# Wider gaps between the background stages of a recurrence kernel: rows stored 4 to 5 tenths of a step ahead of the first pair products, restart slots zeroed behind their last reader

## The chip, the cores and the metric

One core of a Trainium2 chip runs the whole program. The metric is the time of one execution in device microseconds, the median over several runs.

## What is computed

A recurrence over 768 time steps for 32 heads (batch 4 times 8 heads, width 40), then a feed-forward layer:

```python
for t in range(S):
    y[:, :, t] = np.einsum('bhd,bhde->bhe', rt, state)
    Sa = np.einsum('bhde,bhe->bhd', state, at)
    state_decay = state * wt[:, :, None, :] - np.einsum('bhd,bhe->bhde', Sa, bt)
    state = state_decay + np.einsum('bhd,bhe->bhde', vt, kt)
# x: y as (3072 tokens, 320)
h = x @ w_in                                  # 320 -> 2048
g = np.where(h >= 1, h, np.where(h <= -1, 0.0, (h + 1) ** 2 / 4))
return g @ w_out                              # 2048 -> 320
```

All in float32; the layer's matrices are split into a rounded part and a rest, so that its products run on rounded operands.

## The kernel before

The 768 time steps are 24 chunks of 32, and the main loop takes one chunk `c` per step for all heads, in two halves of 16 heads. In a chunk the recurrence is a chain of small products (L488 to L554) with evacuations on VectorE and ScalarE between them. Between the chain's stages the layer for earlier tokens is fed to TensorE: first product (`ph`, L603), gate on ScalarE and VectorE (`gt`, L611 to L613), rounding (`gh`, ScalarE L619) and rest (`gl`, GpSimd L620), second product (`po`, L632), which needs both.

Four chunks make a set `s` (0 to 5). What the chain needs of a set is prepared ahead, in three background stages, for sets 2 to 5 all of them this way:

- **rows** (`prelude`): four parts of 8 time steps. For a part, w is copied into `wz` by ScalarE (L247), whose first and last slot of each row of 10 are zero so that one scan can restart there; GpSimd zeroes them (L246). A forward scan on VectorE (`scan`, L221) gives the running product P, a backward one in `wz` its reciprocal. Into `arena` go P (ScalarE, L257), and by GpSimd a times P (L258), k and b times the reciprocal (L267, L274, called `kt` and `bt`). A DMA from GpSimd's queue stores `arena` in DRAM (`scr`, L275), and the next part writes the same `arena` and the same `wz`. The loads of w, a, k and b (`ld_w` and so on) and the copies of r and v from DRAM to DRAM (`copy_rv`, L129) go through SP's queue.
- **ab** (`ab_set`): for each of the set's chunks the rows of a and b are loaded from `scr` into `tiab` (`load_rows`, L290, four DMAs), transposed by VectorE into `ea` (L304, two calls for each half of the heads), multiplied in pairs on TensorE (L313) and copied to `pairs` by ScalarE (L320). There is one `tiab` and one `ea`: the next chunk's load waits for the last transposes.
- **inv** (`invert`): VectorE transposes `pairs` (L332), GpSimd inverts by 31 pairs of small operations on `lw` (L343, L349), and at a set's start `adopt` transposes the result (`tinv`, L357).

The stages are generators that yield costs. `fill` runs four times per step, each time with six portions of the layer, and behind each portion it calls `background`: 24 slots a step. For each stage and set a table gives a window, in tenths of a step:

```python
rows=[(0, 0), (14, 36), (38, 62), (66, 102), (106, 142)],
ab=[(0, 0), (36, 44), (62, 79), (102, 119), (142, 159)],
```

The first pair is set 1, the last set 5. In a window `background` runs each stage as far as its share of the summed cost is due, the most late first; the first and third `fill` of a step get 1.4 shares, the others 0.6 (`SHARE`). `drain` finishes a stage at once where the next needs it. So `ROWS_W`, `AB_W` and the windows alone set where an instruction stands among the others; every engine and SP's queue then runs its own instructions in that order, each waiting for what it needs. Around the fills SP also gets the main loop's loads (`ti` L290, `cg` L423 and L426) and every second step the relayout of Y into X (L574 to L584).

Of the kernel before, what the change touches and what calls it, by code (L numbers as in the profile page):

```python
# [24 lines left out]


WINDOWS = dict(
    rows=[(0, 0), (14, 36), (38, 62), (66, 102), (106, 142)],
    ab=[(0, 0), (36, 44), (62, 79), (102, 119), (142, 159)],
    inv=[(12, 38), (44, 78), (81, 118), (121, 158), (161, 198)],  # L30
)

SHARE = (1.4, 0.6) * 2
SLOTS = len(SHARE)

ROWS_W = (2, 2, 4, 2, 6, 6, 4)
AB_W = (1, 4, 1, 4, 12, 15)
INV_W = 12

# [11 lines left out]
def rwkv_moe_kernel(ctx: ExitStack, tc: tile.TileContext, r, k, v, w, a, b, w_in, w_out, ident_d, mask_d, out):  # L51
    nc = tc.nc
# [27 lines left out]
    wz = const.tile([128, D, 10], F32, name="wz")  # L80
# [20 lines left out]
    srcs = {n: x.rearrange("b h (c t) e -> (b h) c t e", t=L) for n, x in dict(k=k, w=w, a=a, b=b).items()}  # L101

    nc.gpsimd.memset(dz, 0.0)

    def zero(x, row=0):
        z = zero_c[row : row + x.shape[0]]
        nc.scalar.copy(x, (z if len(x.shape) == 2 else z.unsqueeze(1)).broadcast_to(list(x.shape)))

    def pad_rows(x, n):
        for q in (1, 3):  # L110
            zero(x[32 * q : 32 * q + 32, :, n : n + 32], 32 * q)
# [14 lines left out]
    def copy_rv(s, part, c):  # L126

        x, o = ((r, O_R), (v, O_V))[part]
        nc.sync.dma_start(  # L129
            scr4[s][c, :, :, o : o + D], x.rearrange("b h (n t) e -> (b h) n t e", t=L)[:, 4 * s + c]  # L130
        )

    def pad_scr(s):
        nc.sync.dma_start(scr[s][NH * 128 : NH * 128 + 1, 0:D], r[0, 0, 0:1, :])
# [78 lines left out]
    def scan(out, d0, d1, step=1):  # L213


        def line(x):
            x = x.rearrange("p e t -> p (e t)")
            (pp, pn), (st, n) = x.ap
            return x if step == 1 else bass.AP(x.tensor, x.offset + (n - 1) * st, [[pp, pn], [-st, n]])

        nc.vector.tensor_tensor_scan(  # L221
            out=line(out), data0=line(d0), data1=line(d1), initial=0.0, op0=ALU.mult, op1=ALU.add
        )

    def prelude(s):

        reclaim(8)
        R = arena.rearrange("p (t x) -> p t x", x=160)
        kt, P, at, bt = (R[:, :, 40 * i : 40 * i + 40] for i in range(4))
        rows_ = lambda x: x.rearrange("p e t -> p t e")  # L230

        def load(n, part):
            if n == "w":
                t = work.tile([128, 10 * D], F32, tag="ld_w", name="ld_w")
            else:
                t = work.tile([128, 8 * D], F32, tag="ld_x", name=f"ld_{n}", bufs=2)
            x = t[:, 0 : 8 * D].rearrange("p (t e) -> p t e", e=D)
            nc.sync.dma_start(x, srcs[n][:, 4 * s : 4 * s + 4, 8 * part : 8 * part + 8, :])
            return (t, x) if n == "w" else x

        wl, al, kl = load("w", 0), load("a", 0), load("k", 0)
        pad_scr(s)
        yield 10
        for part in range(4):
            ts_ = slice(8 * part, 8 * part + 8)
            nc.gpsimd.memset(wz[:, :, 0::9], 0.0)  # L246
            nc.scalar.copy(rows_(wz)[:, 1:9], wl[1])  # L247
            yield ROWS_W[0]
            Pc = wl[0].rearrange("p (e t) -> p e t", t=10)
            if part == 0:  # L250
                nc.vector.memset(dz[:, :, 0], -1.0)
            scan(Pc, wz, dz)
            yield ROWS_W[1]
            if part < 3:
                nc.vector.tensor_copy(dz[:, :, 0], Pc[:, :, 8])
            nc.vector.reciprocal(dz[:, :, 9], Pc[:, :, 8])
            nc.scalar.copy(P, rows_(Pc)[:, 1:9])  # L257
            nc.gpsimd.tensor_mul(at, al, rows_(Pc)[:, 0:8])  # L258
            yield 1
            scan(wz, wz, dz, -1)  # L260
            rec = rows_(wz)[:, 2:10]
            for i in range(2):
                copy_rv(s, i, part)
            yield ROWS_W[2]
            bl = load("b", part)
            yield ROWS_W[3]
            nc.gpsimd.tensor_mul(kt, kl, rec)  # L267
            if part < 3:
                wl = load("w", part + 1)
            yield ROWS_W[4]  # L270
            if part < 3:
                al = load("a", part + 1)
            yield ROWS_W[5]
            nc.gpsimd.tensor_mul(bt, bl, rec)  # L274
            nc.gpsimd.dma_start(scr[s][0 : NH * 128, 80:240].rearrange("(p t) x -> p t x", t=L)[:, ts_, :], R)  # L275
            yield ROWS_W[6]
            if part < 3:
                kl = load("k", part + 1)
# [13 lines left out]
    def ab_set(s):  # L292

        if 9 in lending:
            reclaim(9)
            pad_rows(tiab, 48)
        load_rows(tiab, 4 * s, O_A, 80)
        yield AB_W[5]
        for c in range(4 * s, 4 * s + 4):
            tv = tiab.rearrange("p h (j x) -> p h j x", x=40)[:, :, :, 0:32]  # L300
            for half in range(2):
                ea = work.tile([128, 8, 2, 32], F32, tag="ea", name="ea")
                for i in range(2):
                    nc.vector.transpose(ea[:, 4 * i : 4 * i + 4], tv[:, 8 * half + 4 * i : 8 * half + 4 * i + 4])  # L304
                    yield AB_W[0]
                yield AB_W[1]
                ps = psum()[:, 0:128]
                for p in range(8):
                    for f in range(2):
                        rows = slice(64 * f, 64 * f + D)  # L310
                        q = 2 * f + p % 2
                        sl = p // 2
                        nc.tensor.matmul(  # L313
                            ps[32 * q : 32 * q + 32, 32 * sl : 32 * sl + 32],
                            lhsT=ea[rows, p, 0, :], rhs=ea[rows, p, 1, :], start=True, stop=True,
                        )
                assert s - 1 in turned_in
                at = 256 * (c % 4) + 128 * half
                yield AB_W[2]
                nc.scalar.copy(pairs_f[:, at : at + 128], ps)  # L320
                yield AB_W[3]
            if c < 4 * s + 3:
                load_rows(tiab, c + 1, O_A, 80)
                yield AB_W[4]
# [35 lines left out]
    def staged(key, needs, work_of):  # L360
# [13 lines left out]
    done, size, spent = dict(rows=1, ab=1), dict(rows=10 + 4 * (1 + sum(ROWS_W)), ab=AB_W[5] + 3 * AB_W[4] + 8 * (2 * AB_W[0] + sum(AB_W[1:4])), inv=INV_W + 67), {}  # L374
    back = {k: staged(*a) for k, a in dict(
        rows=("rows", None, prelude), ab=("ab", "rows", ab_set), inv=("inv", "ab", invert)).items()}

    def drain(key, s):
# [374 lines left out]
    def reclaim(kind):  # L753

        lending.discard(kind)
        while any(x[0] == kind for x in sts.values()):
            next(wgen)
# [208 lines left out]
```

## Time and profile before

| what | value |
|---|---|
| runs | 988.73 to 993.32 us, median 992.13 |
| the profiled execution: time | 995.83 us |
| its span, first to last instruction | 994.0 us |
| TensorE (PE) busy | 718.4 us, 72% |
| VectorE (DVE) busy | 597.6 us, 60% |
| ScalarE (ACT), GpSimd (POOL) busy | 416.1 us, 435.1 us |
| mean granted clock of TensorE | 0.829 |

Busy shares are means over stages that differ: the start without the layer, the steps with background stages, the last steps with the layer and the chain alone. How long an engine stood before an instruction, and for whom, stands in brackets in the timeline, or summed in the list of waits.

### The profile page before, as it was taken

How to read it: one execution, taken by the hardware profiler on the slowest of the kernel's cores; microseconds unless marked ns; L12 is line 12 of the kernel's file. 1: busy time of each engine (PE TensorE's matmuls, PEld its weight loads, DVE VectorE, ACT ScalarE, POOL GpSimd, SP SyncE). 2: the span in 40 equal slices, each digit the busy share in tenths (PEclk: the TensorE clock that was granted, in tenths of full speed). 3: DMA queues.
4: the chain of work that ended last, by engine and by line, in shares of the span. 5: the costliest groups of instructions: out<-in, count | busy, mean ns of one | idle time of the engine just before them, and what ended most of it. 6: DMA issues, size and time to landing. Idle time of an engine off the chain costs nothing.

```text
span 994.0 us, 34830 instructions
## 1 busy us (share of the span) xinstructions
PE 718.4 (72%) x14976; PEld 647.8 (65%) x14976; DVE 597.6 (60%) x1362; ACT 416.1 (42%) x896; POOL 435.1 (44%) x594
## 2 busy tenths in 40 slices
PE   4442413565776687688786588787799999999995
PEld 3231312454676576577676578676789888899894
DVE  5787777562646555477754486754477767677310
ACT  5543343231323433335433345433245555555552
POOL 3301234883224765435853345855225763222332
PEclk9565555576768788779988799988789999999998
DMA  9399966675557756657646666646535453543000
GB/s 295 68 188 267 228 132 136 165 154 106 90 107 168 142 103 125 115 129 165 143 97 121 116 142 154 141 92 125 104 67 104 85 120 69 127 84 72 17 32 14
DMA packets 223161, 121.97 MB, mean 123 GB/s; under 512 B 142824, under 2 KB 214696, under 8 KB 223008
## 3 DMA queue, kind: packets, MB, share of 16 engines
q1 hardware_dynamic: 219808, 108.61, 52.5%
q0 software_dynamic: 3200, 11.14, 3.6%
q8 instruction: 118, 1.93, 0.9%
q14 instruction: 35, 0.29, 0.1%
HBM read 90.54 MB, written 27.53 MB: 119 GB/s over the span
## 4 chain that ended last, share of the span: by engine, by line
PE 35%; DMA 17%; POOL 14%; DVE 11%; SPq 8%; ACT 7%; issue 7%; POOLq 0%; DVEq 0%; ACTq 0%
PE po L632 12%; PE ph L603 9%; POOL gl L620 5%; DMA scr<-arena 5%; PE p L525 4%; DMA tiab<-scr 4%; SPq L290 3%; PE p L514 3%; DMA ti<-scr 3%; POOL lw L343 3%; POOL lw L349 3%; ACT gh L619 2%; PE p L488 2%; PE p L554 2%; ACT cg L509 1%
## 5 line engine op out<-in xcount | busy, mean ns | idle before, releaser
L620 POOL TENSOR_TENSOR gl<-gt,gh 128x512 fp32r<-128x512 f32 x96 | 123.5, 1286 | 333.3 <-ACT gh L619 333.3
L603 PE MATMUL ph<-X,w 120*128 120x256 f32 x1536 | 223.9, 299 | 9.6 <-DMA X<-Y 4.9
L603 PEld LDWEIGHTS ph<-X,w 120*128 120x128 f32 x1536 | 201.6, 200 | 18.9 <-issue 11.3
L632 PE MATMUL po<-wide,gh 128*128 128x320 f32 x768 | 158.9, 330 | 30.8 <-ACT gh L619 30.8
L632 PEld LDWEIGHTS po<-wide,gh 128*128 128x128 f32 x768 | 127.9, 204 | 33.8 <-ACT gh L619 33.1
L613 DVE SCALAR_TENSOR_TENSOR gt<-gt,ph 128x512 f32<-128x512 f32 x96 | 65.8, 685 | 115.4 <-ACT gt L612 91.2
L632 PE MATMUL po<-wide,gl 128*128 128x320 f32 x384 | 100.1, 345 | 31.8 <-POOL gl L620 31.5
L532 DVE SCALAR_TENSOR_TENSOR cg<-p,pr 40x160 f32<-40x160 f32 x184 | 59.2, 322 | 82.7 <-PE p L525 80.7
L509 ACT ACTIVATE cg<-p 32x160 f32<-32x160 f32 x192 | 56.6, 295 | 106.0 <-PE p L498 78.7
L611 ACT ACTIVATE gt<-ph,half_c 128x512 f32<-128x512 f32 x96 | 66.0, 688 | 80.9 <-PE ph L603 80.8
L632 PEld LDWEIGHTS po<-wide,gl 128*128 128x128 f32 x384 | 68.3, 207 | 42.1 <-POOL gl L620 41.8
L349 POOL TENSOR_TENSOR lw<-lw 128x31 f32<-128x31 f32 (+15 forms) x155 | 90.2, 582 | 8.0
L466 DVE TENSOR_TENSOR cg<-p,mask 32x256 f32<-32x256 f32 x192 | 80.6, 420 | 14.5 <-PE p L457 11.2
L343 POOL TENSOR_TENSOR lw<-lw 128x31 f32<-128x31 f32 (+15 forms) x155 | 82.2, 531 | 8.5
L514 PE MATMUL p<-cg 128*40 128x40 f32 x1472 | 47.0, 231 | 43.4 <-ACT cg L509 43.4
L514 PEld LDWEIGHTS p<-cg 128*40 128x40 f32 x1472 | 40.6, 143 | 54.5 <-ACT cg L509 44.4
L519 ACT COPY ss<-p 40x320 f32<-40x320 f32 x92 | 38.6, 419 | 87.9 <-PE p L514 86.6
L525 PE MATMUL p<-cg 128*64 128x72 f32 (+1 forms) x1536 | 69.7, 253 | 0.2 <-issue 0.2
L505 DVE SCALAR_TENSOR_TENSOR cg<-p,mask 32x128 f32<-32x128 f32 x192 | 55.3, 288 | 16.0 <-ACT cg L509 9.1
L525 PEld LDWEIGHTS p<-cg 128*64 128x64 f32 x1536 | 64.1, 161 | 0.7 <-issue 0.5
L619 ACT CAST gh<-gt 128x512 fp32r<-128x512 f32 x96 | 59.7, 622 | 10.6 <-DVE gt L613 8.6
L313 PE MATMUL p<-ea 40*32 40x32 f32 x1024 | 19.3, 215 | 61.9 <-DVE ea L304 61.5
(108 smaller groups left out, 1083.8 us busy)
## 6 DMA issues: line engine op xcount, KB each, us to landing
ti<-scr SPq DMA_DIRECT2D x96, 200.0 KB
ti<-scr SPq DMA_DIRECT2D x96, 168.0 KB
scr<-arena POOLq DMA_DIRECT2D x16, 640.0 KB, 5.8
cg<-scr SPq DMA_DIRECT2D x96, 80.0 KB
X<-Y SPq DMA_DIRECT2D x36, 160.0 KB
scr<-wide SPq DMA_DIRECT2D x8, 640.0 KB
tiab<-scr SPq DMA_DIRECT2D x32, 160.0 KB
scr<-in_r_dram SPq DMA_DIRECT2D x24, 160.0 KB
```

What stands on the lines that cost most here:

```text
L343: eng.tensor_mul(t3, W3[:, 0:n, j : j + 1].broadcast_to([128, n, m]), L3[:, j + 1 :, j].unsqueeze(1).broadcast_to([128, n, m]),)
L349: eng.tensor_sub(W3[:, 0:n, j + 1 :], W3[:, 0:n, j + 1 :], t3)
L466: nc.vector.tensor_tensor(out=cg[q, f::2, C_X : C_X + 64][:, 4 * i : 4 * i + 4].rearrange("p h (j x) -> p h j x", x=32), in0=ps[quarter(f, ...
L509: nc.scalar.mul(cg[q, f + 2 * j :: 4, C_S : C_S + D], psv[j][quarter(f, j), :, 32:72], -1.0)
L514: nc.tensor.matmul(pst[er[h % 2], h // 2, :], lhsT=cg[:, h, C_S : C_S + D], rhs=cg[:, h, C_G : C_G + D], start=True, stop=True)
L525: nc.tensor.matmul(psv[h // 8][64 * f : 64 * f + 64, h // 2 % 4, 0:n3], lhsT=cgw[:, h * CW + C_G : h * CW + C_G + 64], rhs=cg[:, h, C_R : ...
L603: nc.tensor.matmul(phs[k % 2][:, n * j : n * j + n], lhsT=w1[:, wi, fs], rhs=Xs[g][:, xi, :], start=i == 0, stop=i == 7)
L611: nc.scalar.activation(gt, ph, AF.Relu, bias=half_c, scale=0.5)
L613: nc.vector.scalar_tensor_tensor(out=gt, in0=gt, scalar=1.0, in1=ph, op0=ALU.min, op1=ALU.max)
L619: nc.scalar.copy(gh, gt)
L620: nc.gpsimd.tensor_sub(gl, gt, gh.bitcast(F32))
L632: nc.tensor.matmul(pos[i], lhsT=x[:, ts_], rhs=w, start=at, stop=end)
```

## The change

Four edits. The windows of rows end 3 to 4 tenths of a step earlier, and set 2's also begins 2 earlier; those of ab begin 1 later. The last cost in `ROWS_W`, behind the store, is 8 instead of 4, which makes a set's rows cost 134 instead of 118. The zeroing of `wz` stands behind bt and the store, where `wz` was read last, with one more at the program's start. And the copy to `pairs` follows its products without a yield between.

```diff
--- before.py
+++ after.py
@@ -25,15 +25,15 @@
 
 
 WINDOWS = dict(
-    rows=[(0, 0), (14, 36), (38, 62), (66, 102), (106, 142)],
-    ab=[(0, 0), (36, 44), (62, 79), (102, 119), (142, 159)],
-    inv=[(12, 38), (44, 78), (81, 118), (121, 158), (161, 198)],
+    rows=[(0, 0), (12, 33), (38, 58), (66, 98), (106, 138)],
+    ab=[(0, 0), (37, 46), (63, 79), (103, 119), (143, 159)],
+    inv=[(12, 36), (47, 78), (81, 118), (121, 158), (161, 198)],
 )
 
 SHARE = (1.4, 0.6) * 2
 SLOTS = len(SHARE)
 
-ROWS_W = (2, 2, 4, 2, 6, 6, 4)
+ROWS_W = (2, 2, 4, 2, 6, 6, 8)
 AB_W = (1, 4, 1, 4, 12, 15)
 INV_W = 12
 
@@ -101,6 +101,7 @@
     srcs = {n: x.rearrange("b h (c t) e -> (b h) c t e", t=L) for n, x in dict(k=k, w=w, a=a, b=b).items()}
 
     nc.gpsimd.memset(dz, 0.0)
+    nc.gpsimd.memset(wz[:, :, 0::9], 0.0)
 
     def zero(x, row=0):
         z = zero_c[row : row + x.shape[0]]
@@ -243,7 +244,6 @@
         yield 10
         for part in range(4):
             ts_ = slice(8 * part, 8 * part + 8)
-            nc.gpsimd.memset(wz[:, :, 0::9], 0.0)
             nc.scalar.copy(rows_(wz)[:, 1:9], wl[1])
             yield ROWS_W[0]
             Pc = wl[0].rearrange("p (e t) -> p e t", t=10)
@@ -273,6 +273,7 @@
             yield ROWS_W[5]
             nc.gpsimd.tensor_mul(bt, bl, rec)
             nc.gpsimd.dma_start(scr[s][0 : NH * 128, 80:240].rearrange("(p t) x -> p t x", t=L)[:, ts_, :], R)
+            nc.gpsimd.memset(wz[:, :, 0::9], 0.0)
             yield ROWS_W[6]
             if part < 3:
                 kl = load("k", part + 1)
@@ -316,9 +317,8 @@
                         )
                 assert s - 1 in turned_in
                 at = 256 * (c % 4) + 128 * half
-                yield AB_W[2]
                 nc.scalar.copy(pairs_f[:, at : at + 128], ps)
-                yield AB_W[3]
+                yield AB_W[2] + AB_W[3]
             if c < 4 * s + 3:
                 load_rows(tiab, c + 1, O_A, 80)
                 yield AB_W[4]
```

On GpSimd, in set 3 from the third part's bt to the fourth part's a times P (`arena<-ld_a`; the `lw` rows are the inversion), before:

```order
L274 TENSOR_TENSOR arena_78<-ld_b_3528,wz_79 128x8x40
L275 DMA scr3_103<-arena_78 128x8x160
L343 TENSOR_TENSOR lw_84<-lw_84 128x207
L349 TENSOR_TENSOR lw_84<-lw_84 128x9x23
L246 MEMSET wz_79 128x40x2
L343 TENSOR_TENSOR lw_84<-lw_84 128x220
L349 TENSOR_TENSOR lw_84<-lw_84 128x10x22
L258 TENSOR_TENSOR arena_78<-ld_a_3640,ld_w_3543 128x8x40
```

and after:

```order
L274 TENSOR_TENSOR arena_78<-ld_b_3394,wz_79 128x8x40
L275 DMA scr3_103<-arena_78 128x8x160
L276 MEMSET wz_79 128x40x2
L343 TENSOR_TENSOR lw_84<-lw_84 128x60
L545 TENSOR_TENSOR Y_889<-yt_3325,Y_889 128x2x4x32
L620 TENSOR_TENSOR gl_3523<-gt_3404,gh_3522 128x512
L349 TENSOR_TENSOR lw_84<-lw_84 128x2x30
L343 TENSOR_TENSOR lw_84<-lw_84 128x87
L349 TENSOR_TENSOR lw_84<-lw_84 128x3x29
L258 TENSOR_TENSOR arena_78<-ld_a_3412,ld_w_3402 128x8x40
```

The zeroing stands directly behind the store instead of two inversion operations later, and two products' rests and a copy of Y now lie between the store and the next part's product.

On SP's queue at set 3's first load of `tiab` (`ti` and `cg` are the chain's loads for the next chunks, `X0<-Y` the relayout), before:

```order
L238 DMA ld_b_3804<-in_b_dram 128x1x320
L290 DMA tiab_81<-scr3_103 32x16x80
L290 DMA tiab_81<-scr3_103 32x16x48
L290 DMA tiab_81<-scr3_103 32x16x80
L290 DMA tiab_81<-scr3_103 32x16x48
L290 DMA ti1_83<-scr1_101 32x8x200
L290 DMA ti1_83<-scr1_101 32x8x168
L290 DMA ti1_83<-scr1_101 32x8x200
L290 DMA ti1_83<-scr1_101 32x8x168
L423 DMA cg2_87<-scr1_101 32x8x80
L426 DMA cg2_87<-scr1_101 32x8x40
```

and after:

```order
L291 DMA ti1_83<-scr1_101 32x8x200
L291 DMA ti1_83<-scr1_101 32x8x168
L423 DMA cg2_87<-scr1_101 32x8x80
L426 DMA cg2_87<-scr1_101 32x8x40
L423 DMA cg2_87<-scr1_101 32x8x80
L426 DMA cg2_87<-scr1_101 32x8x40
L291 DMA tiab_81<-scr3_103 32x16x80
L291 DMA tiab_81<-scr3_103 32x16x48
L291 DMA tiab_81<-scr3_103 32x16x80
L291 DMA tiab_81<-scr3_103 32x16x48
L574 DMA X0_1865<-Y_889 40x1024 x3
```

The load of b, the last part's, is no longer ahead of the `tiab` load; the loads of `ti` and `cg` now are, and the relayout follows directly.

On VectorE in set 2, from the second chunk's last transposes to the third chunk's first (each half of a chunk is one `ea` row here; `gt` is the layer's gate), before:

```order
L304 STREAM_TRANSPOSE ea_2660<-tiab_81 128x256 x2
L532 SCALAR_TENSOR_TENSOR cg0_85<-p2_2683,pr1_89 40x4x40 x2
L532 SCALAR_TENSOR_TENSOR cg0_85<-p2_2684,pr1_89 40x4x40 x2
L537 TENSOR_TENSOR yt_2685<-p2_2683,pr1_89 128x128
L537 TENSOR_TENSOR yt_2685<-p2_2684,pr1_89 128x128
L357 STREAM_TRANSPOSE tinv_107<-lw_84 128x32x32
L445 STREAM_TRANSPOSE ev_2728<-ti1_83 128x512
L447 STREAM_TRANSPOSE pr0_88<-ti1_83 128x16x32
L304 STREAM_TRANSPOSE ea_2775<-tiab_81 128x256 x2
```

and after:

```order
L305 STREAM_TRANSPOSE ea_2724<-tiab_81 128x256 x2
L251 MEMSET dz_80 128x40
L222 SCALAR_TENSOR_TENSOR ld_w_2569<-wz_79,dz_80 128x400
L255 COPY dz_80<-ld_w_2569 128x40
L256 RECIPROCAL dz_80<-ld_w_2569 128x40
L222 SCALAR_TENSOR_TENSOR wz_79<-wz_79,dz_80 128x400
L305 STREAM_TRANSPOSE ea_2759<-tiab_81 128x256 x2
L613 SCALAR_TENSOR_TENSOR gt_2764<-gt_2764,ph1_64 128x512
L305 STREAM_TRANSPOSE ea_2807<-tiab_81 128x256 x2
```

Between the last `ea` of the second chunk and the first of the third stood a stage of the chain, the `tinv` transpose and two transposes of the next chunk; now one gate stands there, and scans stand ahead of it.

## Rows read from the trace of the kernel before

**Rows 1.** The page's second part: TensorE's granted clock in 40 slices of 24.85 us, in tenths of full speed (5 is the lower level, 1.2 GHz).

```profile
PEclk9565555576768788779988799988789999999998
```

**Rows 2.** Timeline of VectorE: the `tinv` transposes at the starts of sets 1, 2 and 3 (start us, duration us, engine, line).

```profile
262.02 2.09 DVE L357 STREAM_TRANSPOSE tinv<-lw 128x1024 f32<-128x1024 f32 x1
...
440.50 2.14 DVE L357 STREAM_TRANSPOSE tinv<-lw 128x1024 f32<-128x1024 f32 x1
...
587.80 2.13 DVE L357 STREAM_TRANSPOSE tinv<-lw 128x1024 f32<-128x1024 f32 x1
```

**Rows 3.** The list of waits over the span: who waited for whom, us in total, times, longest us (SPq is SP's DMA queue).

```profile
PE p L313 <- DVE ea L304: 61.5, 17, 11.2
...
DVE ea L304 <- DMA tiab<-scr: 57.9, 12, 9.5
...
ACT arena L257 <- DMA scr<-arena: 29.6, 6, 5.6
...
DVE ld_w L221 <- POOL wz L246: 24.7, 7, 5.9
...
SPq L290 <- DMA scr<-arena: 69.7, 4, 19.1
```

**Rows 4.** Timeline of TensorE in the rows of sets 2 and 3: start us, duration us, and in brackets the time it stood before and for whom. The last row is four products with no gap ahead, for the clock.

```profile
183.36 1.54 PE L514 MATMUL p<-cg 128*40 128x40 f32 x31 [5.76 <-ACT cg L509]
...
221.38 1.43 PE L632 MATMUL po<-wide,gh 128*128 128x320 f32 x4 [6.67 <-ACT gh L619]
224.76 0.90 PE L632 MATMUL po<-wide,gl 128*128 128x320 f32 x2 [1.94 <-POOL gl L620]
...
305.67 1.44 PE L632 MATMUL po<-wide,gh 128*128 128x320 f32 x4 [4.84 <-ACT gh L619]
...
325.32 1.43 PE L632 MATMUL po<-wide,gh 128*128 128x320 f32 x4 [5.37 <-ACT gh L619]
...
346.47 1.44 PE L632 MATMUL po<-wide,gh 128*128 128x320 f32 x4 [6.52 <-ACT gh L619]
...
355.61 0.75 PE L632 MATMUL po<-wide,gh 128*128 128x320 f32 x4
```

**Rows 5.** Timeline of GpSimd, VectorE and ScalarE from the third part's bt of set 3 to the fourth part's copy of P.

```profile
336.00 1.04 POOL L274 TENSOR_TENSOR arena<-ld_b,wz 128x320 f32<-128x320 f32 x1
...
337.33 0.93 POOL L275 DMA_DIRECT2D scr<-arena  x1 [0.30 <-POOL arena L274]
...
339.46 0.21 POOL L246 MEMSET wz<- 128x80 f32 x1
...
339.71 1.31 DVE L221 TENSOR_TENSOR_SCAN ld_w<-wz,dz 128x400 f32<-128x400 f32 x1 [3.50 <-POOL wz L246]
...
343.46 0.77 ACT L257 COPY arena<-ld_w 128x320 f32<-128x320 f32 x1 [5.62 <-DMA scr<-arena]
```

**Rows 6.** The chain of work that ended last: start and length of two stores, from GpSimd's issue to the landing; the first with other transfers beside it, the second nearly alone.

```profile
211.63 6.68 DMA scr<-arena
...
359.25 4.20 DMA scr<-arena
```

**Rows 7.** Timeline around the first loads of `tiab`: set 2's last store, first transposes and first pair products; set 3's load on SP and first transposes; and TensorE's gaps there in sets 3, 4 and 5.

```profile
235.73 0.93 POOL L275 DMA_DIRECT2D scr<-arena  x1 [0.30 <-POOL arena L274]
...
245.25 0.77 DVE L304 STREAM_TRANSPOSE ea<-tiab 128x256 f32<-128x256 f32 x2 [9.50 <-DMA tiab<-scr]
...
245.84 0.68 PE L313 MATMUL p<-ea 40*32 40x32 f32 x32 [11.23 <-DVE ea L304]
...
363.60 1.90 SPq L290 DMA_DIRECT2D tiab<-scr  x4
...
365.10 0.90 PE L632 MATMUL po<-wide,gl 128*128 128x320 f32 x2 [3.71 <-POOL gl L620]
...
368.68 0.77 DVE L304 STREAM_TRANSPOSE ea<-tiab 128x256 f32<-128x256 f32 x2 [5.71 <-DMA tiab<-scr]
...
513.53 0.57 PE L632 MATMUL po<-wide,gl 128*128 128x320 f32 x2 [3.01 <-POOL gl L620]
...
663.46 0.56 PE L632 MATMUL po<-wide,gl 128*128 128x320 f32 x2 [3.48 <-POOL gl L620]
```

**Rows 8.** Timeline at later loads: set 2's third chunk on VectorE; in set 3 SP's relayout and load of the second chunk; TensorE's gaps before the second chunk (sets 3, 4, 5) and the third (set 3, at 406.40).

```profile
265.68 0.77 DVE L304 STREAM_TRANSPOSE ea<-tiab 128x256 f32<-128x256 f32 x2 [0.43 <-DMA tiab<-scr]
...
369.61 2.46 SPq L574 DMA_DIRECT2D X<-Y  x3
...
380.49 2.00 SPq L290 DMA_DIRECT2D tiab<-scr  x4
...
387.01 0.96 PE L313 MATMUL p<-ea 40*32 40x32 f32 x32 [5.68 <-DVE ea L304]
...
406.40 0.68 PE L313 MATMUL p<-ea 40*32 40x32 f32 x32 [7.95 <-DVE ea L304]
...
536.55 0.67 PE L313 MATMUL p<-ea 40*32 40x32 f32 x32 [5.36 <-DVE ea L304]
...
682.74 0.67 PE L313 MATMUL p<-ea 40*32 40x32 f32 x32 [3.33 <-DVE ea L304]
```

**Rows 9.** Timeline: the load of b for set 3's last part on SP, and the bt that uses it on GpSimd.

```profile
346.58 0.58 SPq L238 DMA_DIRECT2D ld_b<-in_b_dram  x1
...
357.91 1.04 POOL L274 TENSOR_TENSOR arena<-ld_b,wz 128x320 f32<-128x320 f32 x1
```

## The prediction

> **What bounds the kernel now.** No engine is full, so I read where each waits. First the granted clock by slices: up to slice 9 (224 us) TensorE is mostly at or near its lower level, then between the two, and from slice 32 on near full [rows 1]. Then the step times: the four chunk steps between the tinv transposes of sets 1 and 2 took 178.5 us, 44.6 each, the next four 147.3, or 36.8 each [rows 2]. A tenth of a step, the unit of WINDOWS, is therefore about 3.7 to 4.5 us, and one of the 24 background slots of a step 1.5 to 1.9 us. Then the list of waits [rows 3]: TensorE stood 61.5 us before the pair products for VectorE's ea, VectorE 57.9 us before the same ea for the tiab load, the SP queue 69.7 us for four stores of rows, ScalarE 29.6 us for six stores to let go of the arena, VectorE 24.7 us for the zeroing of wz on GpSimd. Every queue is in order, so these count only where TensorE stands too, and the timeline of TensorE says where. I look for its gaps there, and sum those that the edits touch.
>
> **Gaps behind the rows of sets 2 and 3.** Six gaps before the second product, 5.76, 6.67, 1.94, 4.84, 5.37 and 6.52 us, are 31.1 us [rows 4]. One of them in full: bt starts on GpSimd at 336.00, the store at 337.33, the zeroing only at 339.46, behind a pair of inversion operations; the forward scan of the next part stood 3.50 us for it; then ScalarE's copy of P stood 5.62 us until 343.46, because P goes into the arena that the store still reads [rows 5]. Everything behind on ScalarE waits too: the rounding gh, and with it TensorE.
>
> After the change the zeroing follows the store directly, so the scan needs no more from GpSimd. And 8 cost units instead of 4 stand behind the store. By the planner's table worked through, in sets 2 and 3 the copy of P stood 2 to 3 slots behind the store of the part before; it will stand 6 to 7. Six slots at 1.5 us are 9 us, or 6.8 at 27 us a step if most stalls vanish; needed are bt's 1.04, 0.3 to the store, and its landing. The landings on the chain were 4.20 us where the store ran alone and 6.68 in traffic [rows 6], so 5.5 to 8.0 us are needed. At the worst 1.2 us per part stay, some 6 us in all: **-25** (bounds 0 and -31). The Trainium skill, page "DMA: Bandwidth & Descriptors", section on the anatomy of one GpSimd DMA, fits 2.0 us plus bytes over 436 GB/s, an estimate of 3.5 us for the 640 KB. No store here was that quick (4.2 us at best), so the trace decides; by the page nothing would stay and the sum would be 6 us better.
>
> **First load of each set.** In set 2 the last store goes at 235.73, ea waits until 245.25, and TensorE stands 11.23 us [rows 7]. The store and the load of tiab are in neighbouring slots, so the load's wait for the landing holds SP, and VectorE behind it. After, set 2's store goes at about 31.7 tenths and the load at 36.7, five tenths or 18 us apart; sets 3 to 5 six to seven apart (56.7 and 62.9 in set 3). The store has long landed. What the load still needs is its own way: 363.60 to 368.68, 5.1 us [rows 7]. SP may send it before its slot is reached, since it then waits for nothing but the DMAs ahead of it: **-10** of the 11.23 (bounds 0 and -11).
>
> In sets 3 to 5 VectorE's first wait lies beside TensorE's work: there TensorE stood 3.71, 3.01 and 3.48 us, for gl on a GpSimd that had just done bt and the store [rows 7]. Those two move away; the lag of the inversion stays, and the same pair now lags elsewhere. I take a bit over half of the 10.2 us: **-6** (bounds 0 and -10).
>
> **Second load of sets 3 to 5.** TensorE stood 5.68, 5.36 and 3.33 us, 14.4 in all, for the second chunk's ea [rows 8]. In set 3 SP sent the relayout of Y only at 369.61, behind the late tiab, ti and cg, then the loads of the next set's rows, and tiab only at 380.49 [rows 8]. Without the stall at the first load SP is some 5 us earlier there, and the second chunk's ea moves three slots back (from 67.5 to 68.75 tenths), about 5 us more. Ten us against the 4 to 6 that lacked: **-12**, 2.4 left (bounds 0 and -14.4).
>
> **Third load.** Here I see no gain. In set 3 TensorE stood 7.95 us [rows 8]; load and ea stay two slots apart. The new order takes scans out from between the two transposes, so that only one gate is cover, but their time falls ahead of the load instead. I take **+3** for sets 3 to 5 (bounds 0 and +12, 4 us of lost cover each). In set 2 that wait was 0.43 us [rows 8] because a whole chain stage and the tinv transpose lay between. Now one gate does, while the fourth chunk, whose wait was a like one, gets the chain stage: about 5 lost, 4 won, **+1**.
>
> **Denser rows.** The windows of rows shrink from 22, 24, 36 and 36 tenths to 21, 20, 32 and 32, and the cost goes from 118 to 134, so between the load of b and its use in bt there are 3 to 4 slots instead of 7 to 8 in sets 2 and 3. The trace shows no wait at bt: the load went at 346.58 and bt ran at 357.91, 11.3 us later [rows 9]. Half of that, 5.6, meets a landing of about 5.1 if I take the tiab load's for it; a wait of 0 to 2 us in eight parts is 0 to 16 us of GpSimd, and I take **+4** on TensorE. The 17 zeroings instead of 16, and the pair copy that loses its one unit of delay, I cost at nothing: ScalarE stands behind the same products either way.
>
> **Clock.** Behind a gap four products took 1.44 us, without one 0.75 [rows 4]. About ten gaps fewer at 0.5 us each: **-5** (bounds 0 and -10).
>
> Sum: -25 -10 -6 -12 +3 +1 +4 -5 = -50. The profiled execution had a span of 994.0 and a time of 995.83; the median of the runs is 992.13, 0.4% less. I subtract from the median: **942**. With every bound at its best -76, or 916; with half the gaps coming back as other waits, -25, or 967.
>
> **The rivals.**
> The stall moves on (0.14): the third load loses its cover fully, 4 us more in each of four sets, and SP, now with the loads of b and w ahead of that tiab load, cures the second load only by half, 6 us less: 942 + 13 + 6 is about 961. For it speaks that VectorE has one gate between the two transposes; against, that the scans only changed sides.
>
> The first load comes late anyway (0.08): in sets 3 to 5 it now stands behind eight ti and cg DMAs, and if SP is held there for the turn that frees ti, the load is issued where it was. Then -10 and -6 fall to a quarter, and -12 to a half: 942 + 12 + 6 = 960.
>
> The store lands sooner once its neighbours are spread (0.08): 4.2 us for all of them [rows 6], nothing left of the 31.1: 936. The page named above points this way.
>
> No change (0.07): TensorE stands at other waits for the same time, since ScalarE's and GpSimd's chain from gate to gl was only hidden behind the stalls: within 5 us of 992. Against it: the four steps with rows but hardly a gap of this kind took 147.3 us where those with them took 178.5 [rows 2].
>
> **Slower** (0.07): bt waits for its load. SP sends b behind the copies of r and v, and where ti and cg loads or the relayout are ahead by 4 us more; landing 5.1 + 4 against 5.6 leaves 3.5 us on GpSimd in each of 16 parts, and gl behind it holds TensorE: 942 + 56 = 998. It decides from about 3.1 us per part on. Against it stands that b is held only by GpSimd's product at, three slots earlier, and that no bt waited before.
>
> **How the numbers follow.** My forecast has 0.56, with a range of its own from 925 to 958. Faster by over 0.5% (5 us, about what a measurement of this kernel can tell from no change): 0.56 + 0.14 + 0.08 + 0.08 = 0.86. Same 0.07, slower 0.07. The range of 918 to 972 takes in the gaining rivals and nearly all bounds of the terms; it leaves out the last two cases and a little of the forecast's tails.
>
> **What would show it.** Right: no wait of ea for the first tiab load in set 2; SP's 69.7 us for stores gone; ScalarE's 29.6 for the arena under 8; VectorE's 24.7 for wz near 0; no gap of over 2 us at the second chunk; steps of sets 1 to 2 near 38 us. A gap of 5 to 8 us at the third chunk of every set stays. Wrong: bt waiting for ld_b on GpSimd, gaps of po for gl where there were none, or the first ea still waiting because SP stood at the ti loads.

## The result, and the profile after

| | before | after |
|---|---|---|
| runs, median | 991.46 us (988.73 to 993.32) | 930.36 us (926.37 to 932.97) |
| ratio, 95% interval | | 0.938 (0.934 to 0.943) |
| span of the profiled execution | 994.0 us | 930.4 us |
| TensorE busy, mean granted clock | 718.4 us, 0.829 | 700.9 us, 0.863 |

The median before is that of four runs; the prediction's 992.13 was the median of three of them. A run of 2069.08 us, one of twelve of the kernel with the zeroing alone moved, is left out of every median and ratio below.

The forecast was 942, its own range 925 to 958. First the granted clock by slices (of 23.3 us) of the page after, against [rows 1]: 24 of the 40 slices stand at 0.9 or more, where 15 did before.

```profile
PEclk9565655666969897899999799899999999999998
```

The list of waits after, against [rows 3]: VectorE's wait for the zeroing and SP's for the store are nearly gone, ScalarE's for the arena is only halved, and bt has a wait that was not there.

```profile
PE p L314 <- DVE ea L305: 30.6, 22, 3.5
...
DVE ea L305 <- DMA tiab<-scr: 19.4, 4, 6.0
...
ACT arena L257 <- DMA scr<-arena: 15.4, 3, 5.9
...
DVE ld_w L222 <- POOL wz L276: 3.0, 1, 3.0
...
SPq L291 <- DMA scr<-arena: 8.8, 1, 8.8
...
POOL arena L274 <- DMA ld_b<-in_b_dram: 5.2, 2, 3.8
```

Where the time went, by stretches from one tinv transpose to the next, first before, then after. A row: stretch, its length, then busy us and instructions of PE, PEld, DVE, ACT and POOL, the granted clock, the DMA share and GB/s. The first row of each runs from a product of the chain that both kernels start at the same time, 227.2 us, to the end of step 3; the others are steps 4 to 7, 8 to 11 and 12 to 15.

```profile
227.20:262.02 34.82, 22.44 (x479) 20.45 (x478) 13.72 (x36) 9.96 (x23) 7.01 (x12) 0.70 0.55 102
262.02:440.50 178.48, 127.92 (x2659) 115.30 (x2658) 99.39 (x228) 64.75 (x142) 83.47 (x115) 0.79 0.61 125
440.50:587.80 147.30, 114.13 (x2497) 103.30 (x2496) 92.26 (x211) 60.55 (x133) 78.33 (x108) 0.90 0.63 130
587.80:732.90 145.10, 121.72 (x2500) 110.56 (x2499) 86.67 (x202) 58.26 (x129) 71.88 (x101) 0.86 0.55 113
```

```profile
227.20:248.58 21.38, 19.37 (x447) 18.05 (x447) 12.06 (x32) 9.69 (x22) 3.29 (x3) 0.83 0.52 103
248.58:410.11 161.53, 127.43 (x2691) 114.55 (x2690) 102.31 (x232) 64.94 (x143) 84.26 (x115) 0.85 0.68 141
410.11:543.13 133.02, 113.07 (x2499) 102.27 (x2498) 91.99 (x211) 60.90 (x133) 77.24 (x108) 0.92 0.67 144
543.13:669.80 126.67, 109.80 (x2499) 99.06 (x2498) 85.86 (x202) 57.94 (x129) 70.06 (x101) 0.96 0.62 128
```

The first four steps gave 13.4 us (262.02 to 248.58), all of it behind 227.2 us; the next three stretches gave 17.0, 14.3 and 18.4. Steps 16 to 19 gave nothing (105.46 and 105.51 us): of the background stages only the last set's inversion runs there, in a window that the change leaves as it was. In steps 12 to 15 two thirds of the gain are not gaps: TensorE was busy 121.7 us before and 109.8 after with the same instructions, at a clock of 0.86 and 0.96.

The gaps of TensorE after that answer to [rows 4], [rows 7] and [rows 8]:

```profile
210.47 1.43 PE L632 MATMUL po<-wide,gh 128*128 128x320 f32 x4 [5.94 <-ACT gh L619]
...
224.80 0.90 PE L632 MATMUL po<-wide,gl 128*128 128x320 f32 x2 [3.67 <-POOL gl L620]
...
241.34 0.68 PE L314 MATMUL p<-ea 40*32 40x32 f32 x32 [2.01 <-DVE ea L305]
...
310.13 0.90 PE L632 MATMUL po<-wide,gl 128*128 128x320 f32 x2 [5.72 <-POOL gl L620]
...
329.11 0.56 PE L632 MATMUL po<-wide,gl 128*128 128x320 f32 x2 [3.85 <-POOL gl L620]
...
351.44 0.56 PE L314 MATMUL p<-ea 40*32 40x32 f32 x32 [0.93 <-DVE ea L305]
...
367.06 0.33 PE L314 MATMUL p<-ea 40*32 40x32 f32 x16 [1.02 <-DVE ea L305]
...
383.47 0.46 PE L314 MATMUL p<-ea 40*32 40x32 f32 x32 [2.40 <-DVE cg L556]
...
463.44 0.90 PE L632 MATMUL po<-wide,gl 128*128 128x320 f32 x2 [3.44 <-POOL gl L620]
...
515.90 0.66 PE L314 MATMUL p<-ea 40*32 40x32 f32 x32 [4.57 <-DVE cg L556]
...
596.97 0.90 PE L632 MATMUL po<-wide,gl 128*128 128x320 f32 x2 [3.92 <-POOL gl L620]
...
645.11 0.54 PE L314 MATMUL p<-ea 40*32 40x32 f32 x32 [2.61 <-DVE cg L556]
```

The first load of set 2 (241.34) and the second chunk of set 3 (367.06) went as forecast, and the third chunk (383.47), from which I expected nothing, fell from 7.95 to 2.40; in sets 4 and 5 (515.90, 645.11) it fell too, from these gaps before:

```profile
555.80 0.67 PE L313 MATMUL p<-ea 40*32 40x32 f32 x32 [7.65 <-DVE ea L304]
...
699.13 0.68 PE L313 MATMUL p<-ea 40*32 40x32 f32 x32 [4.66 <-DVE ea L304]
```

Behind the rows of set 2 (up to 224.80) nothing is won.

### The profile page after: what moved, and what is told of

The parts are those of the page before. It is cut to its first block, busy times and chain, and to the rows that moved or that the text cites. A ratio compares the mean times of both kernels' runs of the same rounds, so it can differ in the third digit from the quotient of the medians.

```text
span 930.4 us, 34829 instructions
## 1 busy us (share of the span) xinstructions
PE 700.9 (75%) x14976; PEld 631.4 (68%) x14976; DVE 597.2 (64%) x1362; ACT 416.0 (45%) x896; POOL 432.9 (47%) x595
## 4 chain that ended last, share of the span: by engine, by line
PE 31%; POOL 10%; DVE 7%; ACT 5%; issue 4%; DMA 2%; SPq 1%; POOLq 0%; DVEq 0%; ACTq 0%
PE po L632 11%; PE ph L603 8%; POOL gl L620 5%; PE p L525 4%; PE p L514 3%; PE p L488 2%; ACT gh L619 2%; PE p L554 2%; DMA tiab<-scr 2%; DVE cg L556 2%; DVE cg L505 1%; POOL lw L343 1%; POOL lw L349 1%; ACT cg L509 1%; ACT gt L611 1%
## 5 line engine op out<-in xcount | busy, mean ns | idle before, releaser
L603 PE MATMUL ph<-X,w 120*128 120x256 f32 x1536 | 220.0, 295 | 1.3 <-issue 0.8
L603 PEld LDWEIGHTS ph<-X,w 120*128 120x128 f32 x1536 | 197.4, 196 | 9.0 <-issue 1.2
L509 ACT ACTIVATE cg<-p 32x160 f32<-32x160 f32 x192 | 56.6, 295 | 112.9 <-PE p L498 69.7
L349 POOL TENSOR_TENSOR lw<-lw 128x31 f32<-128x31 f32 (+15 forms) x155 | 89.8, 579 | 9.1
L343 POOL TENSOR_TENSOR lw<-lw 128x31 f32<-128x31 f32 (+15 forms) x155 | 79.7, 514 | 8.6
L514 PE MATMUL p<-cg 128*40 128x40 f32 x1472 | 44.7, 224 | 43.2 <-ACT cg L509 43.0
L514 PEld LDWEIGHTS p<-cg 128*40 128x40 f32 x1472 | 38.4, 137 | 53.0 <-ACT cg L509 44.0
L525 PE MATMUL p<-cg 128*64 128x72 f32 (+1 forms) x1536 | 66.6, 247 | 0.0
L554 PE MATMUL p<-pr,ss 40*40 40x32 f32 x1472 | 40.6, 208 | 34.5 <-DVE pr L447 28.7
L554 PEld LDWEIGHTS p<-pr,ss 40*40 40x40 f32 x1472 | 35.5, 128 | 43.4 <-issue 19.8
L619 ACT CAST gh<-gt 128x512 fp32r<-128x512 f32 x96 | 59.7, 622 | 10.7 <-DVE gt L613 8.6
L612 ACT ACTIVATE gt<-gt 128x512 f32<-128x512 f32 x96 | 60.6, 632 | 3.0
```

What stands on the lines that cost most here:

```text
L343: eng.tensor_mul(t3, W3[:, 0:n, j : j + 1].broadcast_to([128, n, m]), L3[:, j + 1 :, j].unsqueeze(1).broadcast_to([128, n, m]),)
L349: eng.tensor_sub(W3[:, 0:n, j + 1 :], W3[:, 0:n, j + 1 :], t3)
L509: nc.scalar.mul(cg[q, f + 2 * j :: 4, C_S : C_S + D], psv[j][quarter(f, j), :, 32:72], -1.0)
L514: nc.tensor.matmul(pst[er[h % 2], h // 2, :], lhsT=cg[:, h, C_S : C_S + D], rhs=cg[:, h, C_G : C_G + D], start=True, stop=True)
L525: nc.tensor.matmul(psv[h // 8][64 * f : 64 * f + 64, h // 2 % 4, 0:n3], lhsT=cgw[:, h * CW + C_G : h * CW + C_G + 64], rhs=cg[:, h, C_R : ...
L554: nc.tensor.matmul(psv[er[f], p, :], lhsT=ss[er[f], p, :], rhs=pn[er[f], p, 0, 8:40], start=True, stop=True)
```

## The experiments

Theory A is that of the prediction with its terms re-sized by the trace after; the rivals stand in the expectations. Each ratio is against the kernel before on the same chip.

**The windows alone.** Only the three tables, as in the diff of the change.

> The kernel before with the three changed tables of windows alone; costs, zeroing and the copy to pairs stay as they were. By the table worked through, the copy of P then stands 5 to 6 slots behind the store of the part before in set 2 and 4 to 5 in set 3 (2 to 3 before, 6 to 7 with the whole change), and all of ab stands as in the whole change. Theory A, that the windows bring most: the first load of set 2 (9 us), the second and third loads of sets 3 to 5 (12 and 11 us) and half of what the rows' gaps gave (5 us) go, with some 6 us of clock: about 948, between 938 and 954; VectorE still waits for the zeroing, and ScalarE still for the store in some parts of set 3. Theory B, that zeroing and cost carry the gain, since every engine ran behind the scan that waited: 975 or more.

Measured: 944.66 us, ratio 0.956 (0.951 to 0.960): 4.4% of the 6.2. Theory A holds, B falls. The first load of set 2 has a gap of 1.99 us. What lacks to the whole change is mostly in steps 8 to 11 (143.1 us against 133.0): in set 4 the old cost leaves the copy of P only 4 slots behind the first store, and the rounding gh is late there. Timeline of TensorE:

```profile
448.23 1.44 PE L632 MATMUL po<-wide,gh 128*128 128x320 f32 x4 [7.42 <-ACT gh L619]
```

The three tables changed together, and two windows of the inversion are among them (set 1's ends 2 tenths earlier, set 2's begins 3 later). No run moves these alone, so their part in the 4.4% is not shown.

**Cost and zeroing alone.**

```diff
-ROWS_W = (2, 2, 4, 2, 6, 6, 4)
+ROWS_W = (2, 2, 4, 2, 6, 6, 8)
```

with the zeroing moved as in the change, the windows as before.

> The kernel before with the last cost of rows 8 instead of 4 and the zeroing moved behind the store, windows and copy to pairs as before. The copy of P stands 4 to 5 slots behind the store in sets 2 and 3; the first load of tiab stays 2 slots behind the last store. Theory A: only part of the rows' gaps go (31 us before; the whole change left about 20), so 8 to 15 us, with clock: about 978, between 970 and 986; the 11 us at the first load of set 2 and the 8 us at the third load of set 3 stay in the trace. Theory B (zeroing and cost carry the gain): 950 or less.

Measured: 974.65 us, ratio 0.985 (0.980 to 0.991). As A expected; 4.4% and 1.5% nearly make up the whole. The first load of set 2 and the third chunk of set 3 stall as before (lines are one further down here):

```profile
240.62 0.68 PE L314 MATMUL p<-ea 40*32 40x32 f32 x32 [10.37 <-DVE ea L305]
...
396.46 0.67 PE L314 MATMUL p<-ea 40*32 40x32 f32 x32 [7.67 <-DVE ea L305]
```

**The zeroing alone.** The memset moved behind the store, nothing else.

> The kernel before with the zeroing of wz alone moved. VectorE's 24.7 us of waiting for it should go to near nothing. Theory A: the scan then runs earlier, but the copy of P still waits for the store that reads the arena, in the same place on ScalarE: the same waits with another name, within 4 us of before (987 to 993). Theory B: the scan's lateness was what made the copy late: 10 us or more gained (982 or less).

Measured: 989.60 us, ratio 1.001 (0.998 to 1.005). A holds. The scan still waits for the zeroing, 20.1 us in all, since bt ahead of it is as late as it was; where it comes earlier, ScalarE stands longer for the store. Set 3, third and fourth part, VectorE and ScalarE:

```profile
312.30 1.04 DVE L222 TENSOR_TENSOR_SCAN ld_w<-wz,dz 128x400 f32<-128x400 f32 x1 [1.15 <-POOL wz L276]
...
317.38 0.76 ACT L257 COPY arena<-ld_w 128x320 f32<-128x320 f32 x1 [5.77 <-DMA scr<-arena]
```

**The pair products early again.** The whole change, with ab's windows of before.

```diff
-    ab=[(0, 0), (37, 46), (63, 79), (103, 119), (143, 159)],
+    ab=[(0, 0), (36, 44), (62, 79), (102, 119), (142, 159)],
```

> The whole change, but with the windows of ab as before (they begin and end up to 2 tenths of a step earlier). The last store still stands 10 to 13 slots ahead of the first load of tiab, but the first pair products of the third chunk stand ahead of the chain's stage at 2.5 tenths of the step again, and those of the second chunk about three slots earlier. Theory A, that the third load's gap shrank since the chain's products of that stage now stand on TensorE between load and pair products: gaps of 6 to 8 us at the third chunk of sets 3 to 5 come back, and half of those at the second: 15 us more than the whole change, 940 to 950. Theory C, that SP being early after an unhindered first load made both gaps small: within 4 us of the whole change, 927 to 934.

Measured: 947.09 us, ratio 0.958 (0.953 to 0.963), 2.0 points of the gain lost. A holds, C falls. The third chunks of sets 3 to 5 have 9.19, 8.15 and 5.94 us again (20.3 before, 9.6 with the whole change), the second chunks 1.41, 3.38 and 1.41. TensorE at the third chunk of set 3, here and then in the whole change:

```profile
382.64 0.67 PE L314 MATMUL p<-ea 40*32 40x32 f32 x32 [9.19 <-DVE ea L305]
383.24 1.28 PE L554 MATMUL p<-pr,ss 40*40 40x32 f32 x32
384.45 1.18 PE L498 MATMUL p<-x,tinv 32*32 32x72 f32 x32
```

```profile
377.45 0.80 PE L554 MATMUL p<-pr,ss 40*40 40x32 f32 x32
378.18 0.70 PE L498 MATMUL p<-x,tinv 32*32 32x72 f32 x32
```

In set 2 the gap at the first load stays small here (1.62 us), although its pair products stand where they stood before. So it was not moving them that removed it, nor cost and zeroing, which left 10.37: that leaves the other windows, those of rows first of all. In both kernels set 3's third load stands two slots ahead of ea. But a window that begins one tenth later puts the pair products behind the chain's stage (L554, L498 and on) instead of ahead of it, so the chain runs while the load is under way. The same instructions take 1.28 and 1.18 us behind the gap, 0.80 and 0.70 without.

**b straight into the arena.** The whole change, with four loads into the arena where there was one into a shared tile.

```diff
-            bl = load("b", part)
+            for i in range(4):
+                nc.sync.dma_start(bt[i::4], srcs["b"][:, 4 * s + i, 8 * part : 8 * part + 8, :])
...
-            nc.gpsimd.tensor_mul(bt, bl, rec)
+            nc.gpsimd.tensor_mul(bt, bt, rec)
```

> The whole change, and b is loaded straight into its quarter of the arena (four DMAs, one for each chunk of the set, where there was one into a tile shared with a and k), so that its load no longer waits for GpSimd's product a times P. Theory A, that the 5.72 us gap of TensorE in set 3 and the 5.2 us that bt stood for its load come from that shared tile: both go, and with them the copy of P that then came 5 us too early for the late store; 5 to 9 us less than the whole change, 921 to 926. Theory D, that what counts is the way of the load itself, which now is four DMAs in rows of 160 bytes: bt waits as long or longer, and the time stays at 930 or goes up to 940.

Measured: 935.12 us, ratio 0.947 (0.942 to 0.951), slower than the whole change (0.938, on another chip). D holds: from SP's issue to bt it was 6.6 us (296.05 to 302.69) against 5.4 with the one load (300.09 to 305.49), bt waited 4.97 us where it had waited 3.81, and TensorE's gap was 6.88 us. GpSimd:

```profile
302.69 1.04 POOL L275 TENSOR_TENSOR arena<-arena,wz 128x320 f32<-128x320 f32 x1 [4.97 <-DMA arena<-in_b_dram]
```

**bt on VectorE.** `nc.gpsimd.tensor_mul(bt, ...)` becomes `nc.vector.tensor_mul`.

> The whole change, with the product bt on VectorE instead of GpSimd; the store stays on GpSimd. Theory A, that the gaps of 3.85, 3.44 and 3.92 us behind the last store of sets 3 to 5 come from the 2.2 us of bt, store and zeroing that stand on GpSimd between the rounding gh and the rest gl: each gap shrinks by 1.0 to 1.3 us, and so do like ones of other parts; 3 to 8 us less than the whole change, 922 to 927. Theory E, that GpSimd is late by the whole inversion and not by the rows' operations: the gaps stay within 0.5 us, and the time within 3 us of 930. If VectorE has to wait for the load of b as GpSimd did (5.2 us in set 3), part of the gain goes, and its other work with it: up to 935.

Measured: 925.30 us, ratio 0.938 (0.934 to 0.942), as the whole change. The gaps at the last stores of sets 3 to 5 fall to 3.08, 2.55 and 2.91 us, so GpSimd's bt is in them, as A has it, but the gain in time that A expected did not come. In set 3 the gap of 5.72 us for gl became one of 5.16 for gh, and VectorE pays the rest back at the load of b, 7.4 us at the longest (list of waits):

```profile
DVE arena L274 <- DMA ld_b<-in_b_dram: 15.5, 3, 7.4
```

**Loads of tiab one slot earlier.** `AB_W = (1, 4, 1, 4, 16, 15)`.

> The whole change, with the cost behind a load of tiab 16 instead of 12. The pair products stand where they stood, but the second, third and fourth load of tiab come one slot earlier, three slots ahead of ea instead of two. Theory A, that at the third chunk of sets 3 to 5 the gaps that are left (2.40, 4.57 and 2.61 us) are the load's own way, of which ea still waits 4 to 6 us: they shrink by about the slot's 1.5 us each, 4 to 6 us less than the whole change, 924 to 927. Theory F, that the SP queue sends the load later anyway, since the loads of rows stand ahead of it: no change within 2 us.

Measured: 929.61 us, ratio 0.943 (0.938 to 0.947). A missed, and the loads go as F has it: SP sent the third loads 6.33, 5.98 and 6.52 us ahead of their transposes, no earlier than in the repeat of the whole change below (6.25, 6.49, 6.81). In set 3 the load of b stood on SP just ahead, 2.71 us long. The third chunks' gaps are 1.79, 3.01 and 1.72 us, but those of the second and fourth of sets 3 and 4 rose from 0.9 to 1.8 us to 2.1 to 2.9: the wait moved to its neighbours.

**Set 3's rows in their old window.** `(38, 62)` for `(38, 58)` in rows.

> The whole change, but set 3's rows have their old window, 38 to 62 tenths. Between the load of b and bt are 7 to 8 slots again instead of 3 to 4, between a store and the next copy of P 4 to 5 instead of 6 to 7, and the last store stands 5 slots ahead of the first load of tiab instead of 15. Theory A, that the denser rows cost about what I had put down for them (4 us): bt waits no more and the 5.72 us gap goes, while the copy of P waits 0 to 2 us in each part: 2 to 5 us less than the whole change, 925 to 928, and no wait at the first load. Theory G, that the distance behind the store is what counts: the waits for the store come back with 3 us or more a part, 935 to 942.

Measured: 936.05 us, ratio 0.949 (0.946 to 0.952), slower than the whole change: G holds. bt no longer waits and the first load has no wait with 5 slots, but ScalarE stood 4.97 and 4.34 us for the store again, and gh with it. TensorE in set 3:

```profile
306.71 1.43 PE L632 MATMUL po<-wide,gh 128*128 128x320 f32 x4 [5.27 <-ACT gh L619]
...
325.49 1.36 PE L632 MATMUL po<-wide,gh 128*128 128x320 f32 x4 [3.89 <-ACT gh L619]
```

**The whole change again.**

> The whole change once more, unaltered, so that the next three and the runs so far can be set against it on another chip: ratio to before as it was, 0.938, between 0.934 and 0.943. Its gaps behind the rows of set 3 (5.72 and 3.85 us, both for gl) and at the third chunks (2.4 to 4.6 us) come back within 1 us.

Measured: 926.23 us, ratio 0.936 (0.932 to 0.941); the gaps of set 3 are 5.72 and 3.87 us, the third chunks 2.36, 2.77 and 2.60. Set 4's third chunk had 4.57 the first time, so the 1 us of the expectation does not hold for it: a single gap can differ by 1.8 us from one execution to another.

**The copy to pairs a slot later.** The yield between products and copy put back.

> The whole change, but the copy to pairs stands one slot behind its products again. Theory A, that it is worth nothing (ScalarE stands behind the same products either way): within 2 us of the whole change. Theory H, that ScalarE held by that copy (44.5 us of waits before pairs in the whole change) keeps the gate back: 3 us or more faster with the copy later.

Measured: 927.32 us, ratio 0.937 (0.932 to 0.943). No difference from 926.23 and 0.936 that the runs could tell: A holds, and this edit was rightly costed at nothing.

**Both distances wide in set 3.** `(38, 61)` for `(38, 58)`, and 11 for 8 as the last cost.

> The whole change, with set 3's rows from 38 to 61 tenths instead of 58 and the last cost 11 instead of 8. In set 3 that leaves 5 to 6 slots from the load of b to bt (3 to 4 in the whole change, where bt waited) and 6 to 7 from a store to the copy of P (4 to 5 with the old window and cost 8, where ScalarE waited). Theory A, that both distances were too short and each alone only moved the wait: in set 3 neither bt nor the copy of P waits over 2 us, the 5.72 us gap goes, and the time is 4 to 8 us under the whole change, 0.930 to 0.934 of before. Theory G, that GpSimd's lag behind ScalarE is the wait, whatever the slots: within 2 us of the whole change or slower, gaps of 4 to 6 us stay in set 3.

Measured: 924.58 us, ratio 0.933 (0.926 to 0.939). By the times it is not told apart from the whole change (0.936 beside it). By the trace it does what A says: no bt waits for b, no copy of P waits over 1.6 us in set 3, and steps 4 to 7 took 154.9 us against 159.5 in the repeat. But the profiled execution was the quickest of the four (915.37 us, the others 924.42 to 925.92), so the 154.9 may flatter it. And two gaps of GpSimd's lag stay, this one and one of 3.04 us at 317.47:

```profile
299.86 0.90 PE L632 MATMUL po<-wide,gl 128*128 128x320 f32 x2 [3.94 <-POOL gl L620]
```

**Both, with bt on VectorE.**

> The kernel of the run before with bt on VectorE. With bt on VectorE alone its gaps for gl at the ends of the rows shrank by 0.8 to 1.0 us each, but VectorE stood 15.5 us for the load of b, and the ratio was that of the whole change. Theory A: with 5 to 6 slots between load and bt in set 3 that wait falls to under 8 us and the gain of some 1 us a part stays: 3 to 6 us under the run before, 0.925 to 0.930 of before. Theory G: set 3's gaps stay, 0.935 to 0.940.

Measured: 924.49 us, ratio 0.934 (0.928 to 0.939), nothing beyond the run before. A missed: VectorE still stood 8.9 us for b, where under 8 was expected, and the gain did not come; the time lies just under G's range.

## Why the prediction was right, point by point

The direction came as forecast and the size within its range, and the gaps at the first load of set 2, behind the rows of set 3 and at the second loads shrank about as forecast. Inside the sum three terms were off by more than 10 us, in both directions, and a group of gaps was missing. Gaps are those of TensorE in the profiled executions; the clock's row is its busy time from 227.2 us to the end of step 15.

| term | forecast | trace |
|---|---|---|
| rows of set 2 | part of -25 | the chain's product behind them at 227.19 and 227.23: nothing |
| rows of set 3 | part of -25 | 4.84 + 5.37 + 6.52 gone: -16.7 |
| bt waits for b | +4 | the gap of 5.72: +5.7 |
| first load, set 2 | -10 | 11.23 to 2.01: -9.2 |
| first loads, sets 3 to 5 | -6 | for gl 10.2 to 11.2, for ea none to 6.2: +7.2 |
| second loads, both halves | -12 | 16.0 to 7.3: -8.7 |
| third loads, sets 3 to 5 | +3 | 20.3 to 9.6: -10.7 |
| later chunks, set 2 | +1 | 9.5 to 11.6: +2.1 |
| clock | -5 | 386.2 to 369.7: -16.5 |
| gaps without a releaser | none | 14.1 to 1.0: -13.1 |

These make -59.9; small gaps add -3.2, and -63.1 is the whole difference between 227.2 us and the end of step 15. The terms that came out worse than forecast are 28.4 us off, the better and the missing ones 41.5. That the sum lies only 13 us from the trace (942 against a median of 930.36) is in good part luck. Most of the gaps without a releaser stood before one product of the chain; what they waited for the profile does not show, so their cause stays open (list of waits before; after, that line has none):

```profile
PE p L457 <- issue: 9.7, 6, 2.9
```

Of the signs named ahead, four came: ea does not wait for set 2's first load, SP's 69.7 us for stores fell to 8.8 and VectorE's 24.7 for the zeroing to 3.0, and no gap at the second chunks of sets 3 to 5 is over 2 us. Three did not: ScalarE's wait for the arena is 15.4 us instead of under 8, the steps between sets 1 and 2 took 40.4 us instead of 38, and the third chunks' gaps did not stay. Two signs of being wrong came as well: bt's wait for its load, and a new gap for gl.

**Rows of set 2.** The prediction summed 14.4 us of gaps here, and nothing of it was won: the chain's product behind these rows starts at the same time, before and then after.

```profile
227.19 1.03 PE L514 MATMUL p<-cg 128*40 128x40 f32 x24
```

```profile
227.23 1.03 PE L514 MATMUL p<-cg 128*40 128x40 f32 x24
```

Executions differ by some 5 us up to here: the product starts at 222.41 in the repeat of the whole change, and at 225.19 with the zeroing alone, which gains nothing. (The first of the prediction's six gaps, 5.76 us, stood before a product of the chain and not before the second product.) The step that failed is "six slots at 1.5 us are 9 us". I took the slot's length from steps 4 to 11. In the first two parts of set 2 the layer has not begun (its first product L603 stands at 196.14), and slots without layer work put nothing on ScalarE between the store and the copy of P. GpSimd and ScalarE there, after:

```profile
168.82 0.96 POOL L275 DMA_DIRECT2D scr<-arena  x1 [0.30 <-POOL arena L274]
...
185.04 0.94 POOL L275 DMA_DIRECT2D scr<-arena  x1 [0.30 <-POOL arena L274]
```

```profile
175.23 0.76 ACT L257 COPY arena<-ld_w 128x320 f32<-128x320 f32 x1 [5.90 <-DMA scr<-arena]
...
190.03 0.77 ACT L257 COPY arena<-ld_w 128x320 f32<-128x320 f32 x1 [4.50 <-DMA scr<-arena]
```

ScalarE came to the copy of P at 169.33 and 185.53, half a microsecond behind the store's start, six slots or not. The gap of 5.94 us before gh at 210.47 is not the store's: ScalarE stood 3.81 us before the fourth part's copy of w into `wz`, which bt still read on GpSimd, and then 3.59 for VectorE's scan. The prediction has no term for the wait of that copy for bt, which the change did not remove (list of waits, before and after):

```profile
ACT wz L247 <- POOL arena L274: 17.7, 6, 5.5
```

```profile
ACT wz L247 <- POOL arena L274: 12.7, 4, 4.3
```

For the same reason the scan was not free of GpSimd with the zeroing behind the store: when bt is late, the zeroing is late. All stores after the change landed in 4.2 us at the least and 6.1 at the median, so not all came near 4.2, as one rival had it, and the fit of the Trainium skill (page "DMA: Bandwidth & Descriptors", section on the anatomy of one GpSimd DMA), 3.5 us as an estimate, was not reached.

**Rows of set 3 and b.** Here the mechanism held, and the sum nearly: the three gaps for gh went, and the run with set 3's old window, where two of them came back, shows what the distance behind the store is worth and that a fixed window only trades one distance for the other. One copy of P still stood 5.03 us for a store, which was late because bt had stood 3.81 us for its load; TensorE has no gap behind that copy. The slower rival was thus real in two parts of 16 (3.8 and 1.4 us), and far from 3.1 us in every part.

**First loads of sets 3 to 5.** VectorE's wait for the load went as forecast. The step that failed is "Those two move away": bt and store stand on GpSimd between gh and gl wherever they are, so the gaps for gl came back at the new place, 3.85, 3.44 and 3.92 us; bt on VectorE took 0.8 to 1.0 us out of each. And the pair products of the first chunk, which had no gap of their own before, now have two small ones in each set, 0.93 us (351.44 above) and 1.14 or 1.15, at transposes that VectorE made late without a wait for the load.

**Third loads.** The step that failed is "only one gate is cover". I had followed VectorE, where the transposes lost cover; TensorE gained it, because its pair products moved behind a chain stage. The order of both kernels shows that, and I had looked at the wrong engine in it. With the early windows of ab these gaps are 23.3 us instead of 9.6.

**Clock.** The forecast multiplied ten gaps by what one had cost. The trace shows more: the clock of whole stretches rose. In steps 12 to 15 four runs of the same 2500 products order themselves by it: 121.7 us busy at 0.86 before, 115.4 at 0.91 with cost and zeroing, 112.9 at 0.92 with the windows, 109.8 at 0.96 with the whole change. The two in the middle, in the columns of the stretches above:

```profile
580.74:718.48 137.74, 115.40 (x2499) 104.41 (x2498) 86.20 (x202) 58.11 (x129) 71.59 (x102) 0.91 0.57 119
```

```profile
549.56:681.71 132.15, 112.90 (x2499) 101.56 (x2498) 85.86 (x202) 57.76 (x129) 69.91 (x100) 0.92 0.60 123
```

Fewer gaps and a higher clock come together in these runs; how much of the busy time a single gap costs, none of them separates.

## What to carry to other kernels

A distance in slots of a schedule is a time only where the slots hold work for the engine that has to wait: take the slot's length from the stretch where the instruction stands. When a table moves a product, look at what now stands between the load and that product on the engine that waits, not only on the one that feeds it. And where a gap is removed, count the work behind it at the clock of the better stretch as well; here that was about a quarter of the gain (16.5 of 63.1 us).

## What the runs showed of the hardware

GpSimd's operations and VectorE's scans slow each other, which had no place in my sum. Before the change, on GpSimd, then VectorE twice, the first time with next to no GpSimd operation beside it; and an operation like the first after the change, with no scan beside it:

```profile
485.50 1.27 POOL L349 TENSOR_TENSOR lw<-lw 128x207 f32<-128x207 f32 x1
```

```profile
159.29 0.99 DVE L221 TENSOR_TENSOR_SCAN ld_w<-wz,dz 128x400 f32<-128x400 f32 x1 [0.76 <-POOL wz L246]
...
485.05 1.33 DVE L221 TENSOR_TENSOR_SCAN ld_w<-wz,dz 128x400 f32<-128x400 f32 x1
```

```profile
329.64 0.59 POOL L349 TENSOR_TENSOR lw<-lw 128x207 f32<-128x207 f32 x1
```

The same subtraction took 1.27 us beside a scan and 0.59 without; the scan took 1.33 us where GpSimd's gl still ran at its start (until 485.54), and 0.99 at 159.29. By the Trainium skill, page "SBUF — State Buffer", section "SBUF: two separate sides", of a VectorE operation with two inputs in SBUF and a GpSimd operation that reads SBUF, the one that starts first blocks the other for its whole length. The trace agrees within 0.2 us: from the scan's end at 486.38 another 0.59 us would end at 486.97, and the subtraction ended at 486.77. What this costs the kernel in time no run here separates.
